# Token tiles of the second block loaded before the gated stage and turned in other units, and the two last output steps run tile by tile

## The chip, the cores and the metric

The kernel runs on one core of a Trainium2 chip. The metric is the device time of one execution in microseconds (us); a median of several executions is given. The engines are TensorE (PE, with its weight loads as PEld), VectorE (DVE), ScalarE (ACT), GpSimd (POOL) and SyncE (SP); sixteen DMA engines move data, and each engine's own instructions run in the order in which they were issued.

## The reference

Three stages follow one another, all in float32:

```python
kv  = einsum('bhsd,bhse->bhde', k, v)              # attention without softmax, 8 x 8 x 576 x 64
out = einsum('bhsd,bhde->bhse', q, kv)
x   = out / sqrt(mean(out * out, -1) + 1e-6) * g_norm      # 4608 tokens of 512
# one of 8 experts for each token, F = 1024
out[mask] = gate_w[mask, None] * (relu(x[mask] @ w1[e]) @ w2[e])
# the gated stage, F = 1536
out = (sigmoid(x @ w_gate) * (x @ w_val)) @ w_out
```

The weights of the gated stage come as float64; the kernel reads their bits and makes float32 values of them.

## The kernel before

The first part computes attention and routing, the second the experts. The experts' results go by indirect DMA into the DRAM tensor `y_d`, token rows sorted by expert, each with its token number behind its 512 values; a row has 528 floats. The gate weight of each token stands in `gate_d`.

The third part is the gated stage, from about 650 us to the end. Its tokens are cut into five blocks: block 0 has 4 tiles of 128 tokens (half `h` = 0 only), blocks 1 to 4 have 8 tiles, in two halves of 512 columns. The 1536 gate columns are cut into 12 pieces of 128, so there are 60 *units*: unit `s` is piece `j = s % 12` of block `b = s // 12`. Unit 0 runs at the end of the experts' part, units 1 to 59 in a loop.

A unit of block 0 (`glu_plain`) has two products of 12 matmuls into PSUM banks `gv` (L615 to L617: each product is made of three matmuls of rounded high and low parts), a sigmoid on ScalarE (L621) and a multiplication on VectorE (L627) that leaves `gm`. Between them the function `at(p)` calls `prepare(s, p)` for the *spots* 1, 6, 7 (between the two products) and 2, 5, 4, 3 (after the second); `prepare(s, 0)` comes ahead of the unit. This order, written out by hand, is the order of issue on every engine. At these spots stand:

- spot 0: DMA loads for later units (`load_raw`: the next raw output weights `wo`; `load_rows`: the weights `rows` of unit `s + 2`; `decode_late`: raw float64 weights of 512 KB, for eight units) on SyncE's queue;
- spots 1 and 2: `group`, which splits the weights of unit `s + 1` into high and low parts (ScalarE L603, VectorE L604) and stores them to `wt_d`;
- spot 7: `out_step(s, 0)`, an output step: `gm` of an earlier unit times `w_out`, 4 token tiles of 3 matmuls each (L1140 to L1142), summed in PSUM (`ac`) over the 12 pieces;
- spot 4: `ready_o(s + 1, 0)`, which splits `gm` for the next output step into `gh` (ScalarE L1124) and `gl` (VectorE L1125), in two buffers each;
- spot 3: `decode_late2`, which makes float32 values of late weights on ScalarE and VectorE and stores them (L150, L152).

During each block the tokens of the next one are made ready, tile by tile, in four steps: `load_y` (SyncE, L1160) loads a tile `yr` from `y_d`, into one of four buffers; `number` (GpSimd, L566 and L569) copies its token numbers and gathers the gates from `gate_d`; `weigh` (ScalarE, L573) multiplies the tile with them; `flip` transposes it (TensorE, L578: four transposes) and copies it out of PSUM into `yraw` (ScalarE, L1065). In block 0 two tiles are loaded and numbered in each of units 2 to 5 (spots 0 and 5), weighed and flipped in the unit after that (spots 2 and 4), so in units 3 to 6. In later blocks it is one tile a unit. What uses the finished tokens (`YPLAN`) begins in unit 5.

After unit 59 seven rounds run the output steps that are left, two a round. At a half's last step (`k == 11`) each token tile is copied out of PSUM when its three matmuls are done (ScalarE and VectorE take turns, L1148 and L1146), GpSimd copies its token numbers (`to`, L1150) and scatters the tile to `out` (L1151).

Of the kernel before, what the change touches and what calls it, by code (L numbers as in the profile page):

```python
# [22 lines left out]
HT = 4  # L23
HC = 128 * HT
NB = 5
DM = H * D
# [8 lines left out]
KC = DM // 128  # L35
YW = DM + 16
# [17 lines left out]
def row_of(b, i):  # L54
    return (i + (2 * HT * b - HT if b else 0)) * 128
# [27 lines left out]
def attention_moe_glu_kernel(  # L83
# [4 lines left out]
    nc = tc.nc  # L88
# [70 lines left out]
    with ExitStack() as st:  # L159
# [234 lines left out]
        for b in range(B + 1):  # L394
# [6 lines left out]
            for r in range(5):  # L401
# [34 lines left out]
                elif b > 2:  # L436
                    if r == 1:
                        lane = rank(b // 2 - 2)
                    elif r == 3:
                        lo = lanes(b // 2 - 2, lane)  # L440
# [61 lines left out]
        for t0 in range(0, NTILE, 9):  # L502
# [3 lines left out]
            for t in range(t0, t0 + 9):  # L506
                for w in range(2):
                    nc.tensor.matmul(out=ph[w][:, 0:NSLOT], lhsT=lid[:, t, w, :], rhs=soh[:, t, :],
                                     start=(t == 0), stop=(t == NTILE - 1))
# [49 lines left out]
    oid, gate_t = {}, {}  # L559

    def number(b, i, src):

        if src is not None:
            if i == 0:
                oid[b] = oidp.tile([128, 2 * HT], I32, tag="oid", name="oid")
            nc.gpsimd.tensor_copy(out=oid[b][:, i:i + 1], in_=src[:, DM:DM + 1].bitcast(I32))  # L566
        if i == 0:
            gate_t[b] = oidp.tile([128, 2 * HT], F32, tag="gate", name="gate_t")
        nc.gpsimd.indirect_dma_start(out=gate_t[b][:, i:i + 1], out_offset=None, in_=gate_d[:, :],  # L569
                                     in_offset=bass.IndirectOffsetOnAxis(ap=oid[b][:, i:i + 1], axis=0))  # L570

    def weigh(b, i, src):
        nc.scalar.activation(out=src[:, 0:DM], in_=src[:, 0:DM], func=ACTF.Copy, scale=gate_t[b][:, i:i + 1])  # L573
# [6 lines left out]
    def y_rows(b, i):  # L580
        r = row_of(b, i)
        return y_d[r:r + 128, :]
# [95 lines left out]
    with ExitStack() as st:  # L678
# [165 lines left out]
        at = {}  # L844
# [150 lines left out]
    with ExitStack() as st:  # L995
        ws = st.enter_context(tc.tile_pool(name="g_ws", bufs=2, reuse_waits="tile"))
        yp = st.enter_context(tc.tile_pool(name="g_y", bufs=1, reuse_waits="tile"))
        pgv = st.enter_context(tc.tile_pool(name="g_pgv", bufs=4, space=PSUM, reuse_waits="tile"))
        pac = st.enter_context(tc.tile_pool(name="g_pac", bufs=1, space=PSUM, reuse_waits="tile"))
        NJ = F2 // 128  # L1000
        NU = NB * NJ
# [3 lines left out]
        step_at = {}  # L1005
# [17 lines left out]
        split_o, split_g, acc = {}, {}, {}  # L1023
# [37 lines left out]
        def flip(i, src, ps):  # L1061

            turn(src, ps)
            h, cs = i // HT, slice((i % HT) * 128, (i % HT) * 128 + 128)
            nc.scalar.activation(out=yraw[:, :, h, cs], in_=ps, func=ACTF.Copy)  # L1065

        def load_rows(s):
            if s < 2 * NJ:
                nc.sync.dma_start(out=rows[s % 2], in_=w_rows(s % NJ))
# [40 lines left out]
        def ready_o(s, z):  # L1110


            if (s, z) not in step_at:
                return
            b, h, k = step_at[s, z]
            if b == 0:
                src = raw_o.pop((s, z))
                t = split_o[s, z] = ws.tile([128, 2, DM], F32R, tag="wos", name="wos", bufs=4)
                nc.scalar.activation(out=t[:, 0], in_=src, func=ACTF.Copy)
                nc.vector.tensor_tensor(out=t[:, 1], in0=src, in1=t[:, 0], op=ALU.subtract)  # L1120
                nc.sync.dma_start(out=wo_d[k][:, :, :], in_=t.bitcast(F32))
            src = gms.pop((12 * b + k, h))
            hi, lo = (ws.tile([128, HC], F32R, tag=t, name=t) for t in ("gh", "gl"))
            nc.scalar.activation(out=hi, in_=src, func=ACTF.Copy)  # L1124
            nc.vector.tensor_tensor(out=lo, in0=src, in1=hi, op=ALU.subtract)  # L1125
            split_g[s, z] = (hi, lo)
            free_g.append(src)

        def out_step(s, z):
            if (s, z) not in step_at:  # L1130
                return
            b, h, k = step_at[s, z]
            wos = split_o.pop((s, z))
            wh, wl = wos[:, 0], wos[:, 1]
            gh, gl = split_g.pop((s, z))
            if k == 0:
                acc[b, h] = [pac.tile([128, DM], F32, tag=f"ac{i}", name=f"ac{i}") for i in range(HT)]
            for i in range(HT):
                o, cs = acc[b, h][i], slice(i * 128, i * 128 + 128)
                nc.tensor.matmul(out=o, lhsT=gh[:, cs], rhs=wh, start=(k == 0), stop=False)  # L1140
                nc.tensor.matmul(out=o, lhsT=gh[:, cs], rhs=wl, start=False, stop=False)  # L1141
                nc.tensor.matmul(out=o, lhsT=gl[:, cs], rhs=wh, start=False, stop=(k == NJ - 1))  # L1142
                if k == NJ - 1:
                    ot = yp.tile([128, DM], F32, tag="ot", name="ot", bufs=4)
                    if i % 2:
                        nc.vector.tensor_copy(out=ot, in_=o)  # L1146
                    else:
                        nc.scalar.activation(out=ot, in_=o, func=ACTF.Copy)  # L1148
                    to = yp.tile([128, 1], I32, tag="to", name="to", bufs=4)
                    nc.gpsimd.tensor_copy(out=to, in_=oid[b][:, HT * h + i:HT * h + i + 1])  # L1150
                    put = nc.gpsimd.indirect_dma_start(out=out, out_offset=bass.IndirectOffsetOnAxis(ap=to, axis=0), in_=ot, in_offset=None)  # L1151
                    tc.declare_no_dep(put.ins, group="out", reason="every token has a row of its own")
                    tc.add_to_no_dep_group("out", put.ins)

        yr = {}

        def load_y(b, i):
            if b < NB:
                yr[i] = yp.tile([128, YW], F32, tag="yr", name="yr", bufs=4)
                nc.sync.dma_start(out=yr[i], in_=y_rows(b, i))  # L1160

        late = mw[1].tile([128, 4, 1024], F32, tag="w2r1", name="w2r1")
        jobs = {}
# [28 lines left out]
        def decode_late(s):  # L1192

            for i in ((0, 1) if s == 0 else (s,) if 1 < s < 8 else ()):
                jobs[i] = Late(units[NEARLY + i], i)
# [9 lines left out]
        def prepare(s, spot):  # L1205


            b, j = divmod(s, NJ)
            if spot == 0:
                load_wt(s + 1)  # L1210
                if s + 2 <= NJ:
                    load_raw(s + 2, s + 1)
                load_rows(s + 2)
                decode_late(s)
                sum_w(s + 1)
            if spot == 6:
                ready_o(s, 1)
                load_o(s + 1, 0)
                load_o(s + 1, 1)
            if spot == 1:  # L1220
                group(s + 1, 0)
            if spot == 7:
                out_step(s, 0)
            if spot == 2:
                group(s + 1, 1)
            if spot == 4:
                ready_o(s + 1, 0)
                out_step(s, 1)
            if b + 1 < NB:
                n, j0 = (1, 1) if b else (2, 2)  # L1230
                def turn_at(lo, do):
                    if lo <= j < lo + 2 * HT // n:
                        for i in range(n):
                            do((j - lo) * n + i)
                if spot == 0:
                    turn_at(j0, lambda i: load_y(b + 1, i))
                if spot == 5:
                    turn_at(j0, lambda i: number(b + 1, i, yr[i]))
                if spot == 2:
                    turn_at(j0 + 1, lambda i: weigh(b + 1, i, yr[i]))  # L1240
                if spot == 4:
                    turn_at(j0 + 1, lambda i: flip(i, yr[i], pgv.tile([128, KC, 128], F32, tag="gv", name="tr")))
                if s == 9 and spot == 0:
                    hold_y(mw[1].tile([128, 2, 2, 2, HC], F32R, tag="w2r1", name="w2r1"))
                if s == 11 and spot == 3:
                    hold_y(yA[0][:, 0:2])
                if s == 22 and spot == 1:
                    free_y.append([y0p.tile([128, 2, HC], F32R, tag=f"rows{i}", name=f"rows{i}") for i in range(2)])
                if b and j == NJ - 1 and spot:
                    free_y.append(Y.pop((b, spot)))  # L1250
                for what in YPLAN[min(b, 1)].get((j, spot), ""):
                    y_step(b + 1, what)
            if spot == 3:
                decode_late2(s)
# [3 lines left out]
        late_pool.append(ws)  # L1258
        load_raw(2, 1)
        load_rows(2)  # L1260
        decode_late(0)
        ready_o(1, 0)
        hold_y(yA[0], 2)
        hold_y(mw[1].tile([128, 2, 2, 2, HC], F32R, tag="w1r1", name="w1r1"))
        for s in range(1, NU):
            prepare(s, 0)
            gm = lambda h: gms.setdefault((s, h), free_g.pop(0))
            at = lambda p: prepare(s, p)
# [2 lines left out]
            else:  # L1271
                glu_unit(s // NJ, wts[s % 2], bank, tmp, gm, at)
        for s in range(NU, NU + 7):
            out_step(s, 0)
            ready_o(s, 1)
            load_o(s + 1, 0)
            load_o(s + 1, 1)
            ready_o(s + 1, 0)
            out_step(s, 1)
    y0_scope.close()  # L1280
    mw_scope.close()

# [23 lines left out]
```

## Time and profile before

| | |
|---|---|
| median of 3 runs | 1507.73 us (1506.02 to 1508.78) |
| the profiled execution | 1509.33 us |
| its span, from the first to the last instruction | 1507.5 us |
| mean granted TensorE clock, as a share of the full 2.4 GHz | 0.977 |
| busy: TensorE | 1435.2 us (95%) |
| busy: VectorE, ScalarE, GpSimd | 908.7, 638.5, 228.0 us |
| gated stage | from about 650 us to the end |
| units 1 to 7 of the first block | about 650 to 728 us |

Busy time is summed over a whole kernel of stages with different limits, so the table says only that TensorE has few gaps. Where they lie, and what ends them, is read from the lists of waits and from the order of time of each engine. "[5.20 <-ACT yr L573]" behind an instruction says that its engine stood idle for 5.20 us before it, and that ScalarE's instruction of line 573 ended that. A merged line ("x4") gives the time from the start of the first to the end of the last. Matmuls overlap: a matmul's own duration is longer than the distance between the starts of two.

### The profile page before, as it was taken

The page shows a single profiled execution, that of the slowest core. Times are in us where ns is not written, and L with a number is a line of the kernel's source. Part 1 is how long each engine was busy: PE and PEld are TensorE (multiplying, and loading weights), DVE is VectorE, ACT ScalarE, POOL GpSimd, SP SyncE. Part 2 cuts the span into 40 slices and gives each one's busy share as a digit, 9 for nine tenths or more (in the row PEclk, how much of TensorE's full clock was granted, in tenths as well). Part 3 has the DMA queues.
Part 4 walks back from the last instruction along what each step waited for, and adds up shares of the span by engine and source line. Part 5 has one row for each costly group of instructions (what it writes and reads, how often), then busy time and mean ns, then how long its engine had stood idle before and what let it go on. Part 6 is the DMA issues. An engine that isn't in the chain of part 4 may idle for free.

```text
span 1507.5 us, 22902 instructions
## 1 busy us (share of the span) xinstructions
PE 1435.2 (95%) x8633; PEld 1229.7 (82%) x8633; DVE 908.7 (60%) x1400; ACT 638.5 (42%) x1003; POOL 228.0 (15%) x302
## 2 busy tenths in 40 slices
PE   6984899999999999998999999999999999999997
PEld 5984799999999998776888887888888888888885
DVE  2567788788788887745786676334653436444442
ACT  3756455555555556734443333232322323222221
POOL 1111231222222212202011101011010200101011
PEclk9987799999999999998999999999999999999999
DMA  9976798848886757778797666646465564646444
GB/s 306 325 276 244 196 283 292 293 159 286 285 280 200 248 172 216 267 262 285 266 356 252 243 222 220 238 183 242 177 239 202 206 234 166 246 167 238 177 158 147
DMA packets 154980, 356.31 MB, mean 236 GB/s; under 512 B 20593, under 2 KB 74097, under 8 KB 147697
## 3 DMA queue, kind: packets, MB, share of 16 engines
q1 hardware_dynamic: 140656, 318.17, 60.8%
q0 software_dynamic: 11488, 36.27, 6.9%
q8 instruction: 71, 1.16, 0.3%
q10 hardware_dynamic: 2720, 0.35, 0.2%
q14 instruction: 45, 0.36, 0.1%
HBM read 311.27 MB, written 68.63 MB: 252 GB/s over the span
## 4 chain that ended last, share of the span: by engine, by line
PE 51%; DMA 0%; issue 0%; POOL 0%; DVE 0%; ACT 0%; POOLq 0%; ACTq 0%
PE gv L641 10%; PE gv L643 10%; PE gv L642 10%; PE ac L1142 6%; PE ac L1140 6%; PE ac L1141 6%; PE tr L578 1%; PE gv L615 1%; PE gv L617 1%; PE gv L616 1%; DMA gate_t<-gate_d,oid 0%; POOL out_dram L1151 0%; DVE u L645 0%; POOLq L1302 0%; ACT yr L573 0%
## 5 line engine op out<-in xcount | busy, mean ns | idle before, releaser
L645 DVE TENSOR_TENSOR gm<-u,gv 128x512 f32<-128x512 f32 x96 | 65.8, 686 | 173.5 <-PE gv L643 172.4
L1140 PE MATMUL ac<-wos,gh 128*128 128x512 f32 x432 | 168.6, 390 | 0.0
L1142 PE MATMUL ac<-wos,gl 128*128 128x512 f32 x432 | 168.5, 390 | 0.0
L1141 PE MATMUL ac<-wos,gh 128*128 128x512 f32 x432 | 168.1, 389 | 0.0
L783 PE MATMUL ph<-xh,w1h 128*128 128x256 f32 x576 | 166.9, 290 | 0.8 <-ACT xh L766 0.8
L785 PE MATMUL ph<-xl,w1h 128*128 128x256 f32 x576 | 164.1, 285 | 0.0
L784 PE MATMUL ph<-xh,w1l 128*128 128x256 f32 x576 | 164.0, 285 | 0.0
L665 ACT ACTIVATE s<-gv 128x512 f32<-128x512 f32 x48 | 28.7, 597 | 264.7 <-issue 207.5
L831 PE MATMUL py<-w2l,hh 128*128 128x512 f32 x304 | 119.3, 393 | 0.0
L830 PE MATMUL py<-w2h,hh 128*128 128x512 f32 x304 | 119.3, 392 | 0.0
L832 PE MATMUL py<-w2h,hl 128*128 128x512 f32 x304 | 118.4, 389 | 0.0
L641 PE MATMUL gv<-half,wt 128*128 128x512 f32 x288 | 113.3, 393 | 0.6 <-DVE u L645 0.6
L783 PEld LDWEIGHTS ph<-xh,w1h 128*128 128x128 f32 x576 | 111.3, 193 | 2.5 <-ACT xh L766 1.2
L784 PEld LDWEIGHTS ph<-xh,w1l 128*128 128x128 f32 x576 | 111.4, 193 | 1.5 <-DVE w1l L745 0.2
L643 PE MATMUL gv<-half,wt 128*128 128x512 f32 x288 | 112.4, 390 | 0.0
L642 PE MATMUL gv<-half,wt 128*128 128x512 f32 x288 | 112.1, 389 | 0.0
L785 PEld LDWEIGHTS ph<-xl,w1h 128*128 128x128 f32 x576 | 111.2, 193 | 0.3 <-DVE xl L767 0.3
L645 DVE TENSOR_TENSOR s<-u,gv 128x512 f32<-128x512 f32 x48 | 33.0, 688 | 118.6 <-PE gv L643 118.5
L1151 POOL DMA_INDIRECT out_dram<-ot,to x36 | 37.0, 1028 | 440.6 <-DVE ot L1146 190.6
L1142 PEld LDWEIGHTS ac<-wos,gl 128*128 128x128 f32 x432 | 81.1, 188 | 17.5
L1141 PEld LDWEIGHTS ac<-wos,gh 128*128 128x128 f32 x432 | 81.1, 188 | 17.3
L1140 PEld LDWEIGHTS ac<-wos,gh 128*128 128x128 f32 x432 | 81.1, 188 | 16.8
(273 smaller groups left out, 3333.6 us busy)
## 6 DMA issues: line engine op xcount, KB each, us to landing
wt<-wt_d SPq DMA_DIRECT2D x36, 1536.0 KB
wos<-wo_d SPq DMA_DIRECT2D x96, 512.0 KB
half<-in_moe_w_dram SPq DMA_DIRECT2D x88, 512.0 KB
w1r<-in_moe_w_dram SPq DMA_DIRECT2D x44, 512.0 KB
w2r<-in_moe_w_dram SPq DMA_DIRECT2D x44, 512.0 KB
rows<-w_d SPq DMA_DIRECT2D x24, 512.0 KB
wt<-wt_d SPq DMA_DIRECT2D x48, 256.0 KB
wt_d<-wt SPq DMA_DIRECT2D x12, 1024.0 KB
```

What stands on the lines that cost most here:

```text
L641: nc.tensor.matmul(out=o, lhsT=wh, rhs=yh[:, c, :], start=first and c == 0, stop=False, skip_group_check=True)
L642: nc.tensor.matmul(out=o, lhsT=wh, rhs=yl[:, c, :], start=False, stop=False, skip_group_check=True)
L643: nc.tensor.matmul(out=o, lhsT=wl, rhs=yh[:, c, :], start=False, stop=last and c == 1, skip_group_check=True)
L783: nc.tensor.matmul(out=o, lhsT=bh[:, c, cs], rhs=hi[:, c, 0:n], start=(c == 0), stop=False)
L784: nc.tensor.matmul(out=o, lhsT=bl[:, c, cs], rhs=hi[:, c, 0:n], start=False, stop=False)
L785: nc.tensor.matmul(out=o, lhsT=bh[:, c, cs], rhs=lo[:, c, 0:n], start=False, stop=(c == KC - 1))
L830: nc.tensor.matmul(out=o, lhsT=hi[:, f, cs], rhs=bh[:, f, :], start=first, stop=False)
L831: nc.tensor.matmul(out=o, lhsT=hi[:, f, cs], rhs=bl[:, f, :], start=False, stop=False)
L832: nc.tensor.matmul(out=o, lhsT=lo[:, f, cs], rhs=bh[:, f, :], start=False, stop=last)
L1140: nc.tensor.matmul(out=o, lhsT=gh[:, cs], rhs=wh, start=(k == 0), stop=False)
L1141: nc.tensor.matmul(out=o, lhsT=gh[:, cs], rhs=wl, start=False, stop=False)
L1142: nc.tensor.matmul(out=o, lhsT=gl[:, cs], rhs=wh, start=False, stop=(k == NJ - 1))
```

## The change

1. *First block's turns.* The loads of tiles 0 to 3 of block 1, and then their `number` steps, are issued ahead of the unit loop, behind `load_rows(2)` and ahead of the first late raw loads. Tiles 4, 5 are loaded and numbered in unit 3, tiles 6, 7 in unit 4. Pairs are weighed and flipped in units 2, 3, 5 and 6 (before: 3, 4, 5, 6). A table `TURNS` holds this; its second entry, for the later blocks, has the same turns as before.
2. *The last two output steps.* In the last round both steps' operands are made ready first, and `out_step` takes both: for each token tile the three matmuls of the one and the three of the other. The copies of these four tiles are cut into halves of 256 columns, one on ScalarE and one on VectorE.
3. The `to` copy is issued ahead of the copy out of PSUM, in all blocks.

```diff
+        def store_out(b, h, i, halves):
+            o, ot = acc[b, h][i], yp.tile([128, DM], F32, tag="ot", name="ot", bufs=4)
+            to = yp.tile([128, 1], I32, tag="to", name="to", bufs=4)
+            nc.gpsimd.tensor_copy(out=to, in_=oid[b][:, HT * h + i:HT * h + i + 1])
+            if halves:
+                nc.scalar.activation(out=ot[:, 0:256], in_=o[:, 0:256], func=ACTF.Copy)
+                nc.vector.tensor_copy(out=ot[:, 256:DM], in_=o[:, 256:DM])
...
+        def out_step(*steps):
...
             for i in range(HT):
...
+                for b, h, k, wos, gh, gl in work:
+                    o, cs = acc[b, h][i], slice(i * 128, i * 128 + 128)
+                    wh, wl = wos[:, 0], wos[:, 1]
+                    nc.tensor.matmul(out=o, lhsT=gh[:, cs], rhs=wh, start=(k == 0), stop=False)
+                    nc.tensor.matmul(out=o, lhsT=gh[:, cs], rhs=wl, start=False, stop=False)
+                    nc.tensor.matmul(out=o, lhsT=gl[:, cs], rhs=wh, start=False, stop=(k == NJ - 1))
+                    if k == NJ - 1:
+                        store_out(b, h, i, len(work) > 1)
...
+        TURNS = [{}, {}]
+        for i in range(2 * HT):
+            p = i // 2
+            plan = [((p + 1, 0), load_y), ((p + 1, 5), number_y)] if p > 1 else []
+            for at, what in plan + [((p + 2 + p // 2, 2), weigh_y), ((p + 2 + p // 2, 4), flip_y)]:
+                TURNS[0].setdefault(at, []).append((what, i))
+            for at, what in (((i + 1, 0), load_y), ((i + 1, 5), number_y), ((i + 2, 2), weigh_y), ((i + 2, 4), flip_y)):
+                TURNS[1].setdefault(at, []).append((what, i))
...
             if b + 1 < NB:
-                n, j0 = (1, 1) if b else (2, 2)
-                def turn_at(lo, do):
-                    if lo <= j < lo + 2 * HT // n:
-                        for i in range(n):
-                            do((j - lo) * n + i)
-                if spot == 0:
-                    turn_at(j0, lambda i: load_y(b + 1, i))
-                if spot == 5:
-                    turn_at(j0, lambda i: number(b + 1, i, yr[i]))
-                if spot == 2:
-                    turn_at(j0 + 1, lambda i: weigh(b + 1, i, yr[i]))
-                if spot == 4:
-                    turn_at(j0 + 1, lambda i: flip(i, yr[i], pgv.tile([128, KC, 128], F32, tag="gv", name="tr")))
+                for what, do in TURNS[min(b, 1)].get((j, spot), ()):
+                    what(b + 1, do)
...
         load_raw(2, 1)
         load_rows(2)
+        for i in range(4):
+            load_y(1, i)
+        for i in range(4):
+            number_y(1, i)
         decode_late(0)
         ready_o(1, 0)
...
         for s in range(NU, NU + 7):
-            out_step(s, 0)
+            if s < NU + 6:
+                out_step((s, 0))
             ready_o(s, 1)
             load_o(s + 1, 0)
             load_o(s + 1, 1)
-            ready_o(s + 1, 0)
-            out_step(s, 1)
+            if s == NU + 6:
+                out_step((s, 0), (s, 1))
+            else:
+                ready_o(s + 1, 0)
+                out_step((s, 1))
```

## Rows read from the trace of the kernel before

**Rows 1.** TensorE's waits, 660 us to the end: total us, times, longest.

```profile
PE tr L578 <- ACT yr L573: 10.4, 4, 5.2
```

**Rows 2.** TensorE in order of time: start us, us, engine, line, operation.

```profile
667.18 0.39 PE L615 MATMUL gv<-half,wt 128*128 128x512 f32 x1
...
675.11 0.39 PE L617 MATMUL gv<-half,wt 128*128 128x512 f32 x1
...
688.38 0.40 PE L1140 MATMUL ac<-wos,gh 128*128 128x512 f32 x1
...
693.64 0.40 PE L617 MATMUL gv<-half,wt 128*128 128x512 f32 x1
...
697.48 0.39 PE L1140 MATMUL ac<-wos,gh 128*128 128x512 f32 x1
...
711.75 0.39 PE L617 MATMUL gv<-half,wt 128*128 128x512 f32 x1
...
722.58 0.39 PE L1140 MATMUL ac<-wos,gh 128*128 128x512 f32 x1
```

**Rows 3.** Busy time by stretch; then granted clock, DMA share, GB/s moved.

```profile
652.50:721.00 68.50, 58.13 (x250) 47.23 (x249) 35.93 (x58) 31.32 (x54) 10.88 (x17) 0.88 0.88 308
...
655.00:660.00 5.00, 5.00 (x24) 4.14 (x23) 1.48 (x3) 1.82 (x5) 0.00 (x0) 1.00 0.91 318
...
660.00:665.00 5.00, 5.00 (x24) 4.14 (x23) 4.86 (x9) 3.35 (x6) 0.00 (x0) 1.00 1.02 418
...
685.00:690.00 5.00, 5.00 (x17) 3.96 (x16) 3.14 (x6) 1.64 (x4) 0.97 (x2) 0.71 0.32 109
...
720.00:725.00 5.00, 5.00 (x19) 4.03 (x18) 4.61 (x7) 2.63 (x5) 0.00 (x0) 0.80 0.11 42
```

**Rows 4.** ScalarE in order of time: start us, us, line, operation, idle before.

```profile
654.48 0.60 ACT L621 ACTIVATE s<-gv 128x512 f32<-128x512 f32 x1 [2.42 <-DMA y_d<-y,sidx]
...
663.38 1.16 ACT L603 ACTIVATE wt<-rows 128x512 fp32r<-128x512 f32 x2 [0.79 <-DMA rows<-w_d]
...
668.10 0.63 ACT L1124 ACTIVATE gh<-gm 128x512 fp32r<-128x512 f32 x1 [3.04 <-DVE gm L627]
...
679.93 0.72 ACT L573 ACTIVATE yr<-yr,gate_t 128x512 f32<-128x512 f32 x1 [8.13 <-DMA gate_t<-gate_d,oid]
...
690.18 1.32 ACT L573 ACTIVATE yr<-yr,gate_t 128x512 f32<-128x512 f32 x2
```

**Rows 5.** GpSimd in order of time, columns as before.

```profile
673.48 0.19 POOL L566 COPY oid<-yr 128x1 int32<-128x1 int32 x1 [23.44 <-DMA yr<-y_d]
...
674.22 1.00 POOL L569 DMA_INDIRECT gate_t<-gate_d,oid  x1 [0.55 <-POOL oid L566]
```

**Rows 6.** SyncE's DMA issues in order of time.

```profile
652.28 0.90 SPq L1175 DMA_DIRECT2D w2r<-in_moe_w_val_dram  x2
...
655.29 0.56 SPq L1069 DMA_DIRECT2D rows<-w_d  x1
...
667.04 1.06 SPq L1160 DMA_DIRECT2D yr<-y_d  x2
```

**Rows 7.** The last microseconds, several engines in order of time.

```profile
1491.62 0.63 ACT L1124 ACTIVATE gh<-gm 128x512 fp32r<-128x512 f32 x1 [2.09 <-PE ac L1141]
...
1492.29 0.69 DVE L1125 TENSOR_TENSOR gl<-gm,gh 128x512 fp32r<-128x512 f32 x1 [2.03 <-ACT gh L1124]
...
1496.86 0.39 PE L1142 MATMUL ac<-wos,gl 128*128 128x512 f32 x1
...
1499.54 0.98 POOL L1151 DMA_INDIRECT out_dram<-ot,to  x1 [0.28 <-POOL to L1150]
...
1501.00 0.99 POOL L1151 DMA_INDIRECT out_dram<-ot,to  x1 [0.28 <-POOL to L1150]
```

**Rows 8.** Forms of 128x256 out of PSUM: xcount, busy us, mean ns.

```profile
L792 ACT ACTIVATE hs<-ph 128x256 f32<-128x256 f32 x3 | 1.1, 382 | 0.8 <-PE ph L779 0.8
...
L815 DVE TENSOR_TENSOR hl<-htp,hh 128x256 fp32r<-128x256 f32 x2 | 0.8, 422 | 0.0
```

More of the change, by code (lines that the diff above doesn't have):

```diff
@@ L1127, in ready_o @@
             free_g.append(src)
[L1129 to L1137, printed above, removed]
-            for i in range(HT):
[L1139 to L1153, printed above, removed]
@@ new lines, in store_out @@
+        def store_out(b, h, i, halves):
[5 more added lines that the diff above has]
+                nc.vector.tensor_copy(out=ot[:, 256:DM], in_=o[:, 256:DM])
+            elif i % 2:
+                nc.vector.tensor_copy(out=ot, in_=o)
+            else:
+                nc.scalar.activation(out=ot, in_=o, func=ACTF.Copy)
+            put = nc.gpsimd.indirect_dma_start(out=out, out_offset=bass.IndirectOffsetOnAxis(ap=to, axis=0), in_=ot, in_offset=None)
+            tc.declare_no_dep(put.ins, group="out", reason="every token has a row of its own")
+            tc.add_to_no_dep_group("out", put.ins)
@@ new lines, in out_step @@
+        def out_step(*steps):
+            work = []
+            for sz in steps:
+                if sz in step_at:
+                    b, h, k = step_at[sz]
+                    if k == 0:
+                        acc[b, h] = [pac.tile([128, DM], F32, tag=f"ac{i}", name=f"ac{i}") for i in range(HT)]
+                    work.append((b, h, k, split_o.pop(sz), *split_g.pop(sz)))
+            for i in range(HT):
+                for b, h, k, wos, gh, gl in work:
[6 more added lines that the diff above has]
+                        store_out(b, h, i, len(work) > 1)
@@ L1155, in attention_moe_glu_kernel, with number_y, weigh_y, flip_y @@
         yr = {}
         def load_y(b, i):
-            if b < NB:
-                yr[i] = yp.tile([128, YW], F32, tag="yr", name="yr", bufs=4)
-                nc.sync.dma_start(out=yr[i], in_=y_rows(b, i))
+            yr[i] = yp.tile([128, YW], F32, tag="yr", name="yr", bufs=4)
+            nc.sync.dma_start(out=yr[i], in_=y_rows(b, i))
+        def number_y(b, i):
+            number(b, i, yr[i])
+        def weigh_y(b, i):
+            weigh(b, i, yr[i])
+        def flip_y(b, i):
+            flip(i, yr[i], pgv.tile([128, KC, 128], F32, tag="gv", name="tr"))
@@ L1273, in attention_moe_glu_kernel @@
         for s in range(NU, NU + 7):
-            out_step(s, 0)
+            if s < NU + 6:
+                out_step((s, 0))
             ready_o(s, 1)
@@ L1277, in attention_moe_glu_kernel @@
             load_o(s + 1, 1)
-            ready_o(s + 1, 0)
-            out_step(s, 1)
+            if s == NU + 6:
+                out_step((s, 0), (s, 1))
+            else:
+                ready_o(s + 1, 0)
+                out_step((s, 1))
     y0_scope.close()
```

## The prediction

> **What bounds the kernel now.** I read the page's busy times first: TensorE is busy nearly throughout (table above), so only places where it waits, or runs at half clock, can give much back. The second view is the list of waits of TensorE from 660 us to the end: one line stands out, the transposes of L578 waiting for ScalarE's weighing of `yr`, 10.4 us in four waits [rows 1]. Third, TensorE's own order of time around these waits. In an undisturbed unit with transposes (unit 4), the next output step's first matmul (L1140) starts 3.84 us after the last matmul of the unit's second product: 693.64 to 697.48. In unit 3 the same stretch takes 675.11 to 688.38, 13.27 us, and in unit 6 711.75 to 722.58, 10.83 us [rows 2]. So unit 3 loses 9.43 us and unit 6 loses 6.99 us, **16.4 us together**. That is more than the waits, because after the idle time the granted clock has fallen to the lower level of 1.2 GHz; it is a mean 0.71 even in 685 to 690 us, with TensorE busy throughout [rows 3].
>
> Why the weighing is late stands in three queues [rows 4 to 6]. SyncE issues unit 2's `yr` loads only at 667.04, eight microseconds after the unit began on TensorE, because it issues in order behind stores that wait for VectorE. The tile lands at 673.48 (6.4 us), GpSimd starts the gather of the gates at 674.22, and ScalarE, which wants them in the next unit, can start weighing only at 679.93 (5.7 us later). It stood there from about 671.8. Load and gather take 13 us; the schedule gives them one unit, which without flips is 8.16 us (unit 3, from 667.18 to the end of its second product at 675.11 + 0.23 [rows 2]: 36 matmuls, 0.227 us apart).
>
> **Part 1, the moved loads.** Counts stay: 8 loads, 8 gathers, 8 weighings, 32 transposes. Loads of tiles 0 to 3, and their gathers, go ahead of unit 1; tiles 4 to 7 are loaded in units 3 and 4, two units before their weighing instead of one. Flips go from units 3, 4, 5, 6 to 2, 3, 5, 6.
>
> *What goes:* 16.4 us, if each gate is there when ScalarE comes to it.
>
> *SyncE's queue.* The first `yr` load reads `y_d`, so it waits for the last scatter into `y_d`. That lands by 654.48 at the latest, when ScalarE's wait for it ends [rows 4]; in the kernel before, SyncE had by then issued the two late raw loads (652.28) and went on to the raw and `rows` loads of unit 3 (655.29) [rows 6]. Held 2.2 us, plus four issues of 0.53 us (1.06 for two [rows 6]), everything behind issues about 4.3 us later: two late raw loads, the `wo_d` store, the raw `wo` load and `rows` of unit 3. GpSimd's queue is empty here until 673 [rows 5], so its four early gathers delay nobody. The Trainium skill, page "DMA: Bandwidth & Descriptors", section "Anatomy of one DMA", says that a semaphore wait sits on the issuing sequencer and not in the DMA engines; that rule speaks against this change: by it the 4.3 us count in full; were the wait in the DMA engines, only the DMA time below would. No row of the kernel before shows this load there.
>
> *DMA time.* From 652.5 to 721 the DMA moved 308 GB/s at a share of 0.88, so 21.1 MB at 350 GB/s of full share [rows 3]. Four loads of 264 KB (128 rows of 528 floats) are 1.08 MB, 3.1 us. So unit 3's `rows`, for which ScalarE already waited until 663.38 [rows 4], arrive 3.1 to 3.4 us later, about 666.6. ScalarE splits them in unit 2 (1.2 us), then weighs two tiles (1.32 us for a pair [rows 4]): 669.1, where TensorE wants the flips at 667.2, when unit 2 ends [rows 2]. The gates would be there at or about that time: the load lands at 661 at the latest (6.4 us after its issue, now with less ahead of it, so perhaps at 658), the first two gathers start 0.7 and 2.2 us later, and 5.7 us more give 664.4 to 668.9. Transposes of the second tile then start at 669.1 instead of 667.6: I take **1.5 us of new stall in unit 2**, from 0 (data earlier) to 5.2 and a slow-clock stretch, as in unit 3 now.
>
> *Later units.* Removing the stalls takes away time in which the DMA caught up: at 685 to 690 and 720 to 725 its share is 0.32 and 0.11 [rows 3]. The same 21.1 MB need 60.3 us at full share, to about 713, while TensorE without stalls would begin unit 7's output step 16.4 us before the present 722.58 [rows 2], at 706.2. Now the queue is drained 1.6 us ahead of that step; then it would be 6.8 us behind it. ScalarE has slack: in unit 2 it stood idle 3.04 us before `gh` [rows 4], of which a pair's weighing takes 1.32 us. Up to 713, 4.7 MB (13.5 us) stand in the queue behind unit 7's `rows`, so these are through at 699.5 and land near 701.5 (the same count puts unit 3's at 661.7, and they landed by 663.4 [rows 4]). Split by 702.7 and followed by a pair's weighing, 704.0, they let the flips of unit 6, wanted 3.6 us ahead of the output step at 702.6, end near 704.9 instead of 703.4: 1.5 us, which unit 2's loss already covers, and 0.8 us more for the units between. Residue in all **2.3 us, from 0 to 10**. Part 1: 16.4 - 2.3 = **14.1 us gained**.
>
> The specifications on that skill page give about 358 GB/s of HBM per core: by it 21.1 MB would take 58.9 us, and the residue would be about 1 us. The trace says 350 at full share over the stretch, with one window over the limit (418 GB/s at 660 to 665 [rows 3]), so I stay with the rows.
>
> **Part 2, the last two output steps.** Matmuls stay 24. Now the last step finishes a tile every 0.68 us, and GpSimd needs 1.46 us for each copy-and-scatter pair, so a backlog forms: the last matmul ends at 1496.86 + 0.39 = 1497.25, but the last scatter starts at 1501.00 [rows 7]. With six matmuls a tile (1.36 us) the third scatter is over at 1497.6 or so, and the last one waits only for its copies: halves of 128x256 take 0.38 us on ScalarE and 0.42 on VectorE [rows 8]. Against that: the split of the last `gh` (ScalarE 1491.62, 0.63 us) and `gl` (VectorE 1492.29, 0.69 us) [rows 7] was covered by the twelve matmuls of the step before; now three matmuls cover it, 0.68 us from about 1491.65 (24 matmuls before the end), and `gl`, there at 1492.98, is wanted two matmuls later, at 1492.8: with the weight load, 0.3 us of stall. Last matmul 1497.55, copies 1498.0, scatter about 1498.1: **2.9 us earlier**, from 1.5 (stalls of 1 us, or GpSimd behind) to 3.3 (no stall). The `to` copy, issued ahead of the copies for all blocks, and blocks 1 to 3, whose turns are as before, cost nothing: the same instructions on engines that wait anyway.
>
> **Sum.** 14.1 + 2.9 = 17.0 us. The profiled execution took 1509.33 us, 1.8 around its span and 1.6 over the median: 1492.3 in its terms, **1490.7 us** against the median of 1507.73.
>
> **Rivals.** (a) *The DMA becomes the bound.* For: its share is 0.91 and 1.02 in 655 to 665 [rows 3], before any `yr` load. Against: it reaches 418 GB/s when asked. At 318 GB/s, what it moved in 655 to 660, the 21.1 MB end 6 us later, the residue is 8.3 us and one slow-clock stretch costs 2 more: gain 6.1 + 2.9 = 9, time 1498.7. (b) *The change doesn't get ahead:* the first two gates come after 669, as the load is held by the scatter and the gather takes 5.7 us or more, so unit 2 takes over unit 3's stall (up to 9.4 us) and only unit 6's 7 us go: 7 + 2.9 = 9.9, time 1497.8. For: 664.4 to 668.9 is close to ScalarE's arrival. Against: `rows` come at the same time, so ScalarE isn't there earlier. (c) *Slower:* in units 1 to 6 the DMA, with gathers of four bytes beside full queues, falls below its present rate. At 270 GB/s the 21.1 MB take 78 us, to 730.6, 9.6 us after the present 721; less 2.9 that is 6.7 us slower, 1514.4. It makes the kernel slower from 295 GB/s down, and by over 0.2% from 284. Against: the full stretches read here give 349 GB/s (318 at 0.91) and more at full share [rows 3].
>
> **How the numbers follow.** Forecast 62%, (a) 16%, (b) 14%, (c) 5%, no effect 3%. The range reaches from both stalls fully gone with a full tail gain (16.4 + 3.3: 1488) less a microsecond of spread among runs, 1487, to just past (a): 1499.5. Faster by over 0.2% (3 us, about what a measurement of this kernel can tell from no change) 90%, within 5%, slower 5%.
>
> **What would show it.** Right: the first `yr` loads on SyncE at about 654.5; no wait over 2 us before L578; granted clock 1.00 from 660 to 730; unit 3's `rows` wait moved to about 666.6; unit 7 beginning about 14 us earlier; in the tail a last scatter starting about 1 us behind the last matmul's start, instead of 4.1. Wrong: ScalarE waiting for `gate_t` in unit 2 (b); long waits for `rows` in units 3 to 8 with the DMA share at 1 (a).

## The result and the profile after

Measured on one chip beside the kernel before, the changed kernel takes 1496.59 us (median of 8, 1490.92 to 1499.03) against 1508.26 us (median of 8, 1505.21 to 1515.82). The ratio is 0.9915, with an interval of 0.9892 to 0.9938: by the ratio **12.8 us faster, between 9.4 and 16.3** (the two medians lie 11.7 us apart). The forecast was 17.0 us. The profiled execution took 1494.14 us with a span of 1492.3 us (before 1507.5), at a mean granted clock of 0.984 (before 0.977).

Line numbers have moved: `load_y` is L1166 now, the output step L1156 to L1158, the halves L1134 (ScalarE) and L1135 (VectorE), the scatter to `out` L1140. The waits of the changed kernel from 640 us to the end (waiting engine and line, what for; us in all, times, longest):

```profile
ACT wt L603 <- DMA rows<-w_d: 13.5, 9, 3.3
...
PE tr L578 <- ACT yr L573: 1.7, 1, 1.7
```

The four waits of [rows 1], 10.4 us, are one of 1.7 us, and ScalarE no longer waits for gates anywhere in the first block. Instead it waits nine times for `rows`, 13.5 us in all (before four times, 3.7 us). In order of time, SyncE, GpSimd, ScalarE and TensorE of the changed kernel:

```profile
652.29 0.41 SPq L1069 DMA_DIRECT2D rows<-w_d  x1
654.92 1.75 SPq L1166 DMA_DIRECT2D yr<-y_d  x4
656.71 0.90 SPq L1199 DMA_DIRECT2D w2r<-in_moe_w_val_dram  x2
...
658.12 0.19 POOL L566 COPY oid<-yr 128x1 int32<-128x1 int32 x1 [7.60 <-DMA yr<-y_d]
658.77 0.71 SPq L1069 DMA_DIRECT2D rows<-w_d  x1
658.86 1.00 POOL L569 DMA_INDIRECT gate_t<-gate_d,oid  x1 [0.55 <-POOL oid L566]
...
667.46 0.39 PE L617 MATMUL gv<-half,wt 128*128 128x512 f32 x1
667.71 1.15 ACT L603 ACTIVATE wt<-rows 128x512 fp32r<-128x512 f32 x2 [3.26 <-DMA rows<-w_d]
668.77 1.32 ACT L573 ACTIVATE yr<-yr,gate_t 128x512 f32<-128x512 f32 x2
669.52 1.27 PE L578 MATMUL tr<-ident,yr 128*128 128x128 f32 x8 [1.67 <-ACT yr L573]
...
673.37 0.39 PE L1156 MATMUL ac<-wos,gh 128*128 128x512 f32 x1
...
678.81 1.04 PE L578 MATMUL tr<-ident,yr 128*128 128x128 f32 x8
...
696.03 1.03 PE L578 MATMUL tr<-ident,yr 128*128 128x128 f32 x8
...
705.08 1.04 PE L578 MATMUL tr<-ident,yr 128*128 128x128 f32 x8
...
708.69 0.39 PE L1156 MATMUL ac<-wos,gh 128*128 128x512 f32 x1
```

Read downwards, this is the chain of unit 2. SyncE stands from 652.70 to 654.92, until the scatter into `y_d` has landed. The tiles are then asked for, almost fourteen microseconds before their weighing at 668.77, and the first lands 3.2 us later. The gates are there when ScalarE comes to them (no wait in front of 668.77). But `rows` of unit 3, issued behind the four tiles at 658.77, let ScalarE stand for 3.26 us. Split and weighing follow, and TensorE waits 1.67 us. From the last matmul of the second product to the output step pass 673.37 - 667.46 = 5.91 us where an undisturbed unit takes 3.84 [rows 2]: **2.07 us lost in unit 2**. The flips of units 3, 5 and 6 wait for nothing. Unit 7's output step starts at 708.69 instead of 722.58 [rows 2]; as this execution came 0.48 us later into the stage (last scatter into `y_d` at 649.53, before 649.05), part 1 gave 14.4 us here.

By stretch (start and end, length, busy times of PE, PEld, DVE, ACT and POOL, granted clock, DMA share, GB/s), changed kernel:

```profile
655.00:720.00 65.00, 63.33 (x295) 52.39 (x294) 44.86 (x72) 36.60 (x64) 10.47 (x17) 1.00 0.97 347
...
665.00:670.00 5.00, 3.33 (x17) 2.45 (x15) 3.58 (x7) 2.29 (x5) 0.00 (x0) 1.00 1.03 409
```

The granted clock stays at 1.00, the 2.4 GHz level, even across the 1.67 us wait, so the stretches at 1.2 GHz in [rows 3] are gone too. The tail of the changed kernel, several engines in order of time:

```profile
1477.84 0.39 PE L1156 MATMUL ac<-wos,gh 128*128 128x512 f32 x1
...
1479.23 0.19 PEld L1158 LDWEIGHTS ac<-wos,gl 128*128 128x128 f32 x1 [0.43 <-DVE gl L1125]
...
1480.18 0.42 DVE L1135 COPY ot<-ac 128x256 f32<-128x256 f32 x1 [1.01 <-ACT ot L1134]
1481.39 0.99 POOL L1140 DMA_INDIRECT out_dram<-ot,to  x1 [25.19 <-DVE ot L1135]
...
1482.85 0.99 POOL L1140 DMA_INDIRECT out_dram<-ot,to  x1 [0.28 <-POOL to L1132]
...
1483.45 0.39 PE L1158 MATMUL ac<-wos,gl 128*128 128x512 f32 x1
1483.87 0.38 ACT L1134 ACTIVATE ot<-ac 128x256 f32<-128x256 f32 x1 [0.97 <-PE ac L1158]
1484.29 0.42 DVE L1135 COPY ot<-ac 128x256 f32<-128x256 f32 x1 [0.93 <-ACT ot L1134]
1484.32 0.99 POOL L1140 DMA_INDIRECT out_dram<-ot,to  x1 [0.28 <-issue]
...
1485.78 0.99 POOL L1140 DMA_INDIRECT out_dram<-ot,to  x1 [0.28 <-POOL to L1132]
```

Each VectorE half starts when the ScalarE half has ended (1483.87 + 0.38 = 1484.25, then 1484.29): the halves run one behind the other. And GpSimd is still a chain: the first scatter starts 0.79 us after its data (1480.18 + 0.42 = 1480.60), each next one 1.46 or 1.47 us later, and the last one waits for GpSimd, not for its tile, which was there at 1484.71. It starts 2.33 us behind the start of the last matmul; before it was 4.14 [rows 7]. The `to` copy, issued ahead of the copies now, still runs only when GpSimd has ended the scatter before it, so each round keeps its 1.46 us, as in [rows 7]. The last 24 matmuls, from 1477.84 to 1483.45, take 5.61 us from the first start to the last (before 5.21): 0.40 us of stall, most of it around the wait for `gl`.

### The profile page after: what moved, and what is told of

Same layout as the page of the kernel before. It is cut to its first block, busy times and chain, and to the rows that moved or that the text cites. A ratio compares the mean times of both kernels' runs of the same rounds, so it can differ in the third digit from the quotient of the medians.

```text
span 1492.3 us, 22911 instructions
## 1 busy us (share of the span) xinstructions
PE 1428.2 (96%) x8633; PEld 1223.8 (82%) x8633; DVE 908.8 (61%) x1402; ACT 639.3 (43%) x1005; POOL 225.9 (15%) x302
## 4 chain that ended last, share of the span: by engine, by line
PE 55%; DMA 0%; issue 0%; DVE 0%; POOL 0%; ACT 0%; POOLq 0%
PE gv L641 10%; PE gv L643 10%; PE gv L642 10%; PE ac L1158 6%; PE ac L1156 6%; PE ac L1157 6%; PE gv L617 1%; PE gv L615 1%; PE gv L616 1%; PE tr L578 1%; DMA wt_d<-wt 0%; POOL out_dram L1140 0%; DVE u L645 0%; POOLq L1323 0%; DVE wt L604 0%
## 5 line engine op out<-in xcount | busy, mean ns | idle before, releaser
L1156 PE MATMUL ac<-wos,gh 128*128 128x512 f32 x432 | 168.7, 390 | 0.0
L1158 PE MATMUL ac<-wos,gl 128*128 128x512 f32 x432 | 168.6, 390 | 0.0
L1140 POOL DMA_INDIRECT out_dram<-ot,to x36 | 37.1, 1030 | 439.5 <-DVE ot L1137 190.7
L1158 PEld LDWEIGHTS ac<-wos,gl 128*128 128x128 f32 x432 | 81.1, 188 | 17.8 <-DVE gl L1125 0.4
L1156 PEld LDWEIGHTS ac<-wos,gh 128*128 128x128 f32 x432 | 81.1, 188 | 17.1 <-ACT gh L1124 0.2
```

## Experiments

Executions differ by several microseconds in where the gated stage begins, in code that is the same everywhere: the last scatter into `y_d` starts between 645.06 and 651.16 us in the profiles used here. So beside the ratio I read from each profile the **stretch** from the start of that scatter to the start of the last scatter to `out`: before 851.95, after 836.25 us. It leaves the earlier parts out. Ratios are against the kernel before on the same chip; its medians there were 1507.28, 1511.45 and 1511.23 us.

### The changed kernel again, as a control (no edit)

> The changed kernel again, unchanged, as the control on this chip and to see a second profiled execution. My theory (part 1 gives about 14 us, part 2 about 1.5 us; the residue of part 1 is one stall in unit 2 whose length depends on when unit 3's rows land) expects 12 to 16 us less than the kernel before and, if the execution is a slower one than the first, a longer wait of ScalarE for the rows in unit 2 (first profile: 3.26 us, with 1.67 us of TensorE idle). The rival that the spread of the executions comes from somewhere else expects the same 1.7 us in unit 2 and the difference in another stage.

> The changed kernel once more, as the control for the two below. My theory: the stretch from the last scatter into y_d to the last scatter of the output is 836 to 839 us again, with unit 2's stall between 1.6 and 2.5 us and the granted clock falling only where that wait is over 2 us; the time of the whole moves with the point at which that stretch begins (645 to 651 us so far). The rival that the stretch itself carries the spread expects it to move by as much as the whole time.

| | ratio (interval) | stretch |
|---|---|---|
| first control | 0.9936 (0.9917 to 0.9955) | 839.15 |
| second control, another chip | 0.9889 (0.9861 to 0.9917) | 836.55 |

By these ratios the same kernel gains 9.6 us on one chip, less than the 12 to 16 expected, and 16.8 us on another. In the first control unit 2 shows the second form of its stall. TensorE in order of time, and two stretches (columns as above):

```profile
665.20 0.39 PE L617 MATMUL gv<-half,wt 128*128 128x512 f32 x1
668.05 1.73 PE L578 MATMUL tr<-ident,yr 128*128 128x128 f32 x8 [2.46 <-ACT yr L573]
...
670.86 0.63 PE L615 MATMUL gv<-half,wt 128*128 128x512 f32 x1
671.29 0.63 PE L616 MATMUL gv<-half,wt 128*128 128x512 f32 x1
...
673.42 0.39 PE L1156 MATMUL ac<-wos,gh 128*128 128x512 f32 x1
```

```profile
665.00:670.00 5.00, 2.54 (x12) 1.84 (x11) 3.28 (x6) 3.76 (x7) 0.00 (x0) 0.85 1.03 372
670.00:675.00 5.00, 5.00 (x19) 4.03 (x18) 3.56 (x7) 2.50 (x6) 0.00 (x0) 0.81 1.00 359
```

After a wait of 2.46 us the granted clock falls to the lower level for a while: matmuls start 0.43 us apart instead of 0.227, and the stretch lasts 8.22 us, a loss of 4.38 instead of 2.07. The wait itself is 0.8 us longer, the clock makes up the other 1.5 us. In the second control the wait is 1.61 us, the clock stays at 1.00, and unit 2 loses 2.05 us.

### Each part alone

Only the loads (the last round as before):

```diff
-            if s < NU + 6:
-                out_step((s, 0))
+            out_step((s, 0))
...
-            if s == NU + 6:
-                out_step((s, 0), (s, 1))
-            else:
-                ready_o(s + 1, 0)
-                out_step((s, 1))
+            ready_o(s + 1, 0)
+            out_step((s, 1))
```

> The moved loads and turns alone; the last two output steps as before. My theory: 1.4 us slower than the changed kernel, 11 to 14 us faster than before; the same stall in unit 2 (ScalarE waits about 3 us for rows, TensorE about 1.7 us). If the tail gave the larger share, it would be 3 us slower than the changed kernel.

Only the tail (turns as before):

```diff
-            plan = [((p + 1, 0), load_y), ((p + 1, 5), number_y)] if p > 1 else []
-            for at, what in plan + [((p + 2 + p // 2, 2), weigh_y), ((p + 2 + p // 2, 4), flip_y)]:
+            for at, what in (((p + 2, 0), load_y), ((p + 2, 5), number_y), ((p + 3, 2), weigh_y), ((p + 3, 4), flip_y)):
...
-        for i in range(4):
-            load_y(1, i)
-        for i in range(4):
-            number_y(1, i)
```

> The two last output steps tile by tile, with the loads and turns of the kernel before. My theory: units 3 and 6 lose 9 and 7 us as before, and the tail gives about 1.4 us: the last scatter starts 2.3 us behind the start of the last matmul instead of 4.1, and 0.4 us of stall appear in the merged step. The prediction's own figure was 2.9 us, with the scatter 1 us behind.

The loads alone give a ratio of 0.9949 (0.9930 to 0.9969), 7.7 us where 11 to 14 were expected, and a stretch of 837.49; the last scatter stands 4.13 us behind the last matmul's start, as in the kernel before. The tail alone gives 0.9979 (0.9954 to 1.0003), an interval that takes in no change, and 847.24, with 2.32 us at the end. So part 1 carries most of the gain. What part 2 gives can't be told from the times; by the rows of the tail it is 1.4 us (worked out below), and the stretches with and without it (837.49 against 836.25 and 836.55, where unit 2's stall is as short) differ by 0.9 to 1.2. The run with the tail alone keeps the late gates, in unit 3, a little in unit 5 (0.78 us) and again in unit 6 (TensorE in order of time):

```profile
680.23 1.11 PE L578 MATMUL tr<-ident,yr 128*128 128x128 f32 x4 [5.42 <-ACT yr L573]
...
715.14 0.66 PE L578 MATMUL tr<-ident,yr 128*128 128x128 f32 x4 [2.29 <-ACT yr L573]
```

Behind the second wait the clock kept its level here, and unit 6 lost 2.9 us instead of the 6.99 read from [rows 2]. The stretch is 4.71 us below that of the kernel before, 1.41 of which is the tail: in this execution the old stalls cost about 3.3 us less than in the one that the prediction read.

### Whole copies in the tail

```diff
-                        store_out(b, h, i, len(work) > 1)
+                        store_out(b, h, i, False)
```

> The changed kernel with whole copies of 512 columns in the last two steps, ScalarE and VectorE in turn, instead of halves. My theory (the second half waits for the first, so a tile takes 0.8 us by halves and 0.6 to 0.7 whole; GpSimd's scatters follow one another every 1.47 us from the first one on): the first scatter starts 0.2 us earlier after its tile, and so does the last: 0.2 us less between the last matmul and the last scatter. The rival that halves save time (0.4 us a tile side by side) expects 0.3 us more there.

Ratio 0.9912 (0.9877 to 0.9948). The last matmul starts at 1482.91, the last two rows of the tail are:

```profile
1483.54 0.99 POOL L1140 DMA_INDIRECT out_dram<-ot,to  x1 [0.28 <-issue]
...
1485.00 0.99 POOL L1140 DMA_INDIRECT out_dram<-ot,to  x1 [0.28 <-POOL to L1132]
```

That is 2.09 us, 0.24 less than with halves. One ScalarE copy of 128x512 takes 0.60 us, the two halves 0.84 in sequence; the first tile, from which GpSimd's chain counts, is ready that much sooner. The halves cost a little, they don't help; the two runs below that also have whole copies show 2.09 and 2.10 us.

This kernel is the changed one up to its last steps, and its unit 2 takes the stall in the second form again, behind a shorter wait than in the first control:

```profile
667.44 1.73 PE L578 MATMUL tr<-ident,yr 128*128 128x128 f32 x8 [2.37 <-ACT yr L573]
```

The granted clock is 0.78 from 665 to 670 us and 0.88 from 670 to 675, and the unit loses 4.27 us. Of the five profiles with these loads and turns (the changed kernel's three, the loads alone with 1.94 us lost, and this one), two lose over 4 us in unit 2 and three about 2.

### What holds unit 2 up

Two tiles ahead of the unit loop instead of four; tiles 2 and 3 at unit 1's spots 0 and 5, behind `rows` of unit 3 (`number_y` likewise):

```diff
-            plan = [((p + 1, 0), load_y), ((p + 1, 5), number_y)] if p > 1 else []
+            plan = [((p + 1, 0), load_y), ((p + 1, 5), number_y)] if p > 1 else [((1, 0), load_y), ((1, 5), number_y)] if p else []
...
-        for i in range(4):
+        for i in range(2):
```

> Only tiles 0 and 1 are loaded ahead of the unit loop; tiles 2 and 3 in unit 1, behind unit 3's rows in SyncE's queue. Half the data and half the issues stand ahead of these rows. My theory (the rows are late because the tile loads stand ahead of them): the rows land about 1.5 to 2.6 us earlier, ScalarE's wait for them in unit 2 falls from 3.3 to about 1 us, TensorE's stall there from 1.7 us to near 0; 1.5 us faster than the changed kernel, if the gates are in time. The rival that unit 2's stall is the gates' lateness expects no change of the stall.

The raw `wo` load and `rows` of unit 3 ahead of the tiles:

```diff
-                if s + 2 <= NJ:
+                if s > 1 and s + 2 <= NJ:
                     load_raw(s + 2, s + 1)
-                load_rows(s + 2)
+                if s > 1:
+                    load_rows(s + 2)
...
+        load_raw(3, 2)
+        load_rows(3)
         for i in range(4):
             load_y(1, i)
```

> The raw output weights and the rows of unit 3 are issued ahead of the four tile loads, in the time in which SyncE waits for the scatter. My theory: ScalarE's wait for rows in unit 2 vanishes, but the tiles land about 2 us later (0.79 MB ahead of them, at 350 GB/s), so the gates of tiles 0 and 1 come at about 667 to 670 and ScalarE may wait for the gates instead: a stall of 0 to 2.5 us in unit 2, within 1 us of the changed kernel. If the rows were not what holds the flips, nothing would change.

Flips in units 3 to 6 as before, four tiles loaded ahead all the same, the others in spot 3:

```diff
-            plan = [((p + 1, 0), load_y), ((p + 1, 5), number_y)] if p > 1 else []
-            for at, what in plan + [((p + 2 + p // 2, 2), weigh_y), ((p + 2 + p // 2, 4), flip_y)]:
+            plan = [((p + 1, 3), load_y), ((p + 1, 3), number_y)] if p > 1 else []
+            for at, what in plan + [((p + 3, 2), weigh_y), ((p + 3, 4), flip_y)]:
```

> The loads ahead as in the changed kernel, but the flips in units 3, 4, 5, 6 as in the kernel before; tiles 4 to 7 are loaded at the end of units 3 and 4, when their buffers are free. My theory: no flips wait for rows in unit 2, but rows that land 18 us after the last scatter into y_d are also late for unit 3's own first product (their split ends some 1.3 us after unit 2's products), so TensorE waits for the weights there instead, 1 to 2 us: within 1 us of the changed kernel. The rival that the flips' place alone makes the stall expects no stall at all and 2 us less.

| | ratio (interval) | stretch | TensorE waits for L573 | `rows` of unit 3 split, from the `y_d` scatter |
|---|---|---|---|---|
| after and its two controls | 0.9915, 0.9936, 0.9889 | 836.25, 839.15, 836.55 | 1.7, 2.5, 1.6 | 18.18, 19.52, 18.49 |
| two tiles ahead | 0.9913 (0.9892 to 0.9934) | 835.22 | 0.6 | 16.95 |
| `rows` first | 0.9919 (0.9898 to 0.9939) | 835.62 | 0.4 | 16.33, no wait |
| flips stay | 0.9897 (0.9851 to 0.9943) | 839.08 | 1.3 (two, later units) | 20.22 |

With two loads less in front of it `rows` come 1.2 to 2.6 us earlier and TensorE's wait shrinks by about a microsecond or more. ScalarE's wait for them doesn't shrink as expected (to 1 us): it is 3.56 us, as ScalarE comes to them earlier too. With `rows` first they don't hold ScalarE at all, and the gates just begin to. ScalarE with `rows` first:

```profile
666.16 1.14 ACT L603 ACTIVATE wt<-rows 128x512 fp32r<-128x512 f32 x2
667.87 0.72 ACT L573 ACTIVATE yr<-yr,gate_t 128x512 f32<-128x512 f32 x1 [0.58 <-DMA gate_t<-gate_d,oid]
669.12 0.72 ACT L573 ACTIVATE yr<-yr,gate_t 128x512 f32<-128x512 f32 x1 [0.52 <-DMA gate_t<-gate_d,oid]
```

So the stall of unit 2 is `rows` behind the tile loads, not late gates. Leaving the flips where they were doesn't avoid it. TensorE then has no flips in unit 2, runs on, and stops at unit 3's first matmul, which needs the split weights:

```profile
672.07 0.50 PE L615 MATMUL gv<-half,wt 128*128 128x512 f32 x1 [2.43 <-ACT wt L603]
```

The granted clock is 1.00 from 670 to 675 us in this run, behind a wait as long as that of the first control (2.46 us) and longer than that of the run with whole copies (2.37 us), behind which it fell.

The first two ratios overlap that of the control on their chip, and the third, on a chip without a control of its own, those of both: a microsecond of stretch is at the edge of what the times can show, so the verdicts here rest on the waits.

### The pieces put together

`rows` first, flips in units 3 to 6 and whole copies:

> Three edits together: rows and raw weights of unit 3 ahead of the tile loads, flips in units 3 to 6, whole copies in the tail. My theory: rows come in time and no flip stands in unit 2, so neither unit 2 nor unit 3 has a wait of TensorE, and the granted clock stays 1.00 from the start of the gated stage on: 2 to 3 us less than the changed kernel in the stretch from the last scatter into y_d to the last scatter of the output (836 to 839 us in the changed kernel's two profiles), about 833.5. If the DMA were the bound in these units, the wait would come up again in a later unit and the stretch would stay at 836.

`rows` first, two tiles ahead and whole copies:

> Only tiles 0 and 1 ahead of the loop, tiles 2 and 3 in unit 1; raw weights and rows of unit 3 ahead of them all; flips as in the changed kernel; whole copies in the tail. My theory: neither rows nor gates hold the flips of unit 2 by more than 0.5 us; the stretch from scatter to scatter takes 834 to 835 us, 2 to 4 us less than the changed kernel. If the DMA were the bound of these units, the order of the loads would not matter and it would stay at 836 or more.

The edits are those shown above. The first gives 0.9902 (0.9866 to 0.9939) and a stretch of 836.89, no better than the change itself. TensorE there, in unit 5:

```profile
695.93 0.66 PE L578 MATMUL tr<-ident,yr 128*128 128x128 f32 x4 [0.44 <-ACT yr L573]
697.38 0.66 PE L578 MATMUL tr<-ident,yr 128*128 128x128 f32 x4 [0.79 <-ACT yr L573]
```

ScalarE waits 0.72 us for the second tile's gate there: with the loads of tiles 4 to 7 in spot 3 instead of spot 0, gates are late again, now in unit 5. The second gives 0.9883 (0.9859 to 0.9908), beside 0.9889 for the control on the same chip, and a stretch of 835.18: one wait of 1.0 us is left (0.5 expected), for the gates. Its stretch is 1.1 to 4.0 us below those of the changed kernel, its time can't be told from it.

### More for the DMA to do

A load of 512 KB that nothing reads, in each of units 1 to 6 (3.1 MB), computation unchanged:

```diff
+                if 1 <= s <= 6:
+                    spare = ws.tile([128, 4, 256], F32, tag="wsum", name="wsum", bufs=1)
+                    nc.sync.dma_start(out=spare, in_=w_rows(s))
```

> The changed kernel with one more load of 512 KB in each of units 1 to 6, into a buffer that is not in use there; no result depends on it. That is 1.5 us of DMA time for each unit at 350 GB/s. My theory (the DMA runs at its full rate from unit 1 to unit 6, and what kept it off the critical path is a backlog of some 7 us that the units' slack just covers): the rows come later from unit to unit and TensorE waits for weights or flips in several of units 2 to 8, 4 to 10 us in all. The rival that the DMA has room left expects less than 1 us.

Ratio 0.9870 (0.9831 to 0.9909, from two executions only), stretch 837.51: at most 1.3 us more than the two profiles of the changed kernel without the lower clock, not 4 to 10. The second control, whose last scatter into `y_d` started at nearly the same time (645.15 and 645.06), and this run, in the same 65 us:

```profile
655.00:720.00 65.00, 63.39 (x296) 52.38 (x295) 47.10 (x76) 36.04 (x63) 10.10 (x16) 1.00 0.98 353
...
655.00:720.00 65.00, 62.73 (x289) 50.99 (x288) 46.66 (x75) 35.53 (x61) 11.61 (x16) 1.00 1.03 391
```

TensorE waited 1.21, 0.47 and 0.60 us for the weighing, ScalarE 21.2 us for `rows` in ten waits. The DMA moved 391 GB/s where the changed kernel, at a share of 0.98, moved 353. A busy share near 1 was no sign here that its capacity was used up.

## Why the prediction was right, and where it was too high

The direction held, the time lies in the range, and the forecast's mechanism is the one seen; two sizes were off. The range took in the rivals (a) and (b) as well, and the measured 1496.59 lies nearer to their 1498.7 and 1497.8 than to the forecast 1490.7: it is the waits that tell them apart, not the time.

| step | forecast | measured |
|---|---|---|
| late gates in units 3 and 6 | 16.4 us go | gone: no wait for gates in the first block |
| first `yr` load on SyncE | 654.5 | 654.92 |
| first tile lands | 658 to 661 | 658.12 |
| `rows` of unit 3 arrive | 666.6 (3.1 to 3.4 us later) | 667.7 (3.85 us later, counted from the scatter) |
| new stall in unit 2 | 1.5 us (0 to 5.2) | about 2 in three profiles, over 4 in two |
| further loss in later units | 0.8 us | none seen |
| part 1, to unit 7's output step | 14.1 us | 14.4; in the four other profiles 14.5, 14.0, 11.8, 11.4 |
| last scatter behind last matmul's start | about 1 us | 2.33 us |
| stall in the merged step | 0.3 us | 0.40 us |
| part 2 | 2.9 us (1.5 to 3.3) | 1.41 us |

**Part 1** went as reckoned in its mechanism, for the reason given. The waits for `rows` move to where the loads were put in front of them, the gates come about when ScalarE does, and the experiments with two tiles and with `rows` first show the stall's cause by moving it. The prediction left open whether what stands behind the held load counts its 4.3 us in full and reckoned with the DMA time of the tiles alone, 3.1 to 3.4 us. The two late raw loads issued 4.4 us later than before (656.71 against 652.28) and `rows` 3.5 us (658.77 against 655.29), so the wait did sit on SyncE, and `rows` came 3.85 us later from the scatter (18.18 against 14.33): 0.6 us more than forecast, about what the stall of 2.07 us has over its 1.5. Two things were missing. The stall of unit 2 has two sizes, with the clock kept or lost, and the forecast took the small one: that part 1 came out at 14.4 in the profile shown, so near the 14.1, is in part luck of that execution. And 16.4 us was read from one execution, in which both old stalls had pulled the clock down. With the tail alone the old stalls cost about 3.3 us less. Taking the changed kernel's stretch as the mean of its three profiles, 837.3, part 1 and 2 together are worth 851.95 - 837.3 = 14.6 us against the profiled execution of before, and 847.24 + 1.41 - 837.3 = 11.4 us against one with the stalls of the run with the tail alone. The measured 12.8 lies between. That the stalls of before vary this way over its executions is argued from two profiles, not shown; it would also explain part of the span between 9.6 and 16.8 us on two chips.

**Part 2** is the term that was mis-sized. The last scatter comes 4.14 - 2.33 = 1.81 us nearer to the last matmul, less 0.40 of stall: 1.41 us. The step that failed is "the third scatter is over at 1497.6 or so, and the last one waits only for its copies". It counted GpSimd's pace from the tiles, one in 1.36 us; but GpSimd needs 1.46 us a scatter whatever the tiles do, and the chain starts 0.79 us behind the first tile's data, so GpSimd is still at its third scatter when the last tile is ready. The trace of the kernel before showed that start already, 0.77 us behind the copy's end at 1495.25 + 0.60:

```profile
1495.25 0.60 ACT L1148 ACTIVATE ot<-ac 128x512 f32<-128x512 f32 x1 [3.00 <-PE ac L1142]
...
1496.62 0.99 POOL L1151 DMA_INDIRECT out_dram<-ot,to  x1 [26.62 <-ACT ot L1148]
```

And the prediction took the halves to run side by side, 0.42 us, where they ran in sequence, 0.84. The Trainium skill, page "PSUM — Partial Sum Buffer", section "PSUM bank collisions raise a hardware error", speaks against this part, and the prediction missed it: two engines must not access the same PSUM bank and 32-partition quadrant at once, two reads included, and the compiler's scheduler puts a dependency between them. The trace agrees: all four VectorE halves start 0.02 to 0.04 us after the ScalarE half ends. Whether the order comes from the bank or from the shared tile `ot` wasn't tried apart.

**The rivals.** The residue in later units was priced with "350 GB/s of full share", (a) with 318 and (c) with 270. The chip moved 391 over 65 us when more was queued, so 350 was no ceiling; nothing of the DMA-bound cases was seen. The Trainium skill, page "Perfetto Trace Analysis", section "Roofline", says that 358 GB/s is a core's part when both cores of a pair draw on the memory, and that one core alone can go about 20% over it; 391 over 65 us, 1.09 of it, agrees. (b) didn't happen: the gates were in time. By how much is not shown: the run with `rows` first has waits of 0.58 and 0.52 us for them, but there the tiles stand behind `rows`, and the first gather is issued 12 instead of 9 us after the scatter.

**Still open.** What moves the start of the gated stage by 6 us between executions was not tried; it lies ahead of all that the change touches, and over the changed kernel's three profiles it moves by 4.4 us, the stretch by 2.9. Whether it makes up most of the spread of the times is not shown. How often unit 2 takes the stall with the clock down is known from five profiles only, two of which have it.

## What to carry to other kernels

A load moved ahead pays with whatever stands behind it in its queue: look there first, and count with the chance that a new wait of 2 us also costs the clock (4.38 us lost instead of 2.07). Read a stall's price from more than one execution, over a stretch between two events of the kernel's own, when the work ahead of it varies by more than the change is worth. At an end where one engine issues the last transfers one by one, count that engine's own pace and its start, not the pace at which work reaches it; and look whether the halves of a copy out of one PSUM bank run side by side at all before cutting it between two engines: here they never did.

## What the runs showed of the hardware that I had not expected

- **DMA.** 391 GB/s over 65 us at a share of 1.03, against 347 and 353 at 0.97 and 0.98 and 308 at 0.88 [rows 3]: the rate rose by more than the share.
- **A load's latency depends on what is queued.** The first `yr` load landed 3.2 us after its issue (654.92 to 658.12); with the raw weights and `rows` of unit 3 issued ahead of it 5.2 us (655.80 to 660.96); in the kernel before, issued at 667.04 with the DMA share near 1, 6.4 us [rows 5, 6].
- **GpSimd's scatter** starts 0.79 us after its data are there when the engine has stood idle, and then every 1.46 us (0.99 for the issue, 0.19 for the copy, 0.28 between).
- **The clock** stayed at 2.4 GHz behind TensorE's waits of 1.67, 2.29 and 2.43 us and fell to 1.2 GHz behind waits of 2.37 and 2.46 us, with TensorE busy before each. The length of the wait alone doesn't tell them apart, nor did it keep to the 2 us that the second control's expectation supposed; what does was not tried.
